# Moving start-up work between ScalarE and VectorE, and within VectorE's queue, in a transform-and-feed-forward kernel

## Chip, core, metric

The kernel runs on one core of a Trainium2 chip. The metric is the device time of one execution in microseconds (us). The kernel before takes 629.54 us (median of three runs, 629.07 to 629.83). In the views of the profile PE is TensorE's matmuls, PEld its weight loads, DVE is VectorE, ACT ScalarE, POOL GpSimd, and SP the engine that issues most DMAs. "L216" is line 216 of the kernel; the changed kernel's lines are about four higher than those of the kernel before.

## The reference

```
def _attn_ref(x):                       # x: 8 x 3008 x 256
    X = np.fft.fft(x, axis=1)
    X = np.fft.fft(X, axis=2)
    return X.real
def _moe_ref(x, w_gate, w_val, w_out):  # 24064 x 256, d_ff 1536
    gate = np.maximum(x @ w_gate, 0.0)
    val = x @ w_val
    return gate * val @ w_out
```

## The kernel before

The sequence transform is split into 94 x 32. For each of 8 batches, stage 1 multiplies by tables over 94 points, a turn brings the data onto other partitions, and stage 2 multiplies by tables over 32 points and yields `pq`. The transform over 256 columns is folded into the weights (`wc`, `ws`, `wm`), so that the main loop of 288 steps (8 batches, 3 blocks, 12 slices of d_ff) is gate, value, product and output matmuls. Batch 0 goes a special way, because nothing is there yet that could hide its start: its rows are multiplied as they land (`first_products`), with VectorE or ScalarE making the reversed copies (`ends`, `back`).

```python
def first_products(c, upper, k):            # row pair c, lower or upper x, straight or reversed copy
    ...
        nc.tensor.matmul(o, lhsT=lhs, rhs=other if k != upper else same, ...)                  # L216
        if jj == 0:                                                                           # self-paired row
            nc.tensor.matmul(psf[c][0:1, 384:480], lhsT=lhs[:, 0:1], rhs=..., ...)              # L219
...
pl.tensor_scalar(perm[:], dd[:], scalar1=mi[:], scalar2=None, op0=ALU.is_equal)   # POOL reads dd
...
jj, sl, up, odd = bits(0, 15), bits(4, 1), bits(5, 3), bits(0, 1)                 # DVE, 8 tiny ones
z = col("z", ...); nz = ...; mul = ...; o0 = ...; o1 = ...                        # DVE, 7 tiny ones
...
ends(24, 8); back(25, 3, "act"); back(28, 3, "dve"); ...                          # turn of the upper x
group((1, 2, 3), True)                                                            # PE: second half of rows 1 to 3
ends(8, 4); back(8, 4, "act")
dve.tensor_scalar(dd[:], dd[:], scalar1=mi[:], ...); residue(dd[:], dq[:], D, dve)
first_evac(2, "act"); first_evac(1, "dve"); first_evac(3, "dve")
...
fold_w(0, 0, 0, g_tile()); upright(0, 0, "act"); upright(0, 1, "dve")
fold_w(0, 0, 1, g_tile())                     # ends with the scaling of wm on DVE
rotate(0, 0, 4, dve.tensor_copy)
stage2(0, 0, 0, "act"); fold_w(0, 1, 0, g_tile()); stage2(0, 0, 1, "dve"); fold_w(0, 1, 1)
```

The remaining weight folds, and the uprights, rotations and stage 2 pieces of batch 0's blocks 1 and 2, are hung onto main-loop steps 1 to 10. They share two PSUM buffers in turn.

Of the kernel before, what the change touches and what calls it, by code (L numbers as in the profile page):

```python
# [11 lines left out]
F32 = mybir.dt.float32  # L12
# [32 lines left out]
def kernel(ctx: ExitStack, tc, x, w_gate, w_val, w_out, out):  # L45
# [9 lines left out]
    NKA = 12  # L55
# [136 lines left out]
    def back(r, n, evac):  # L192

        dst = tabs["back"][:, r:r + n, 1:H]
        src = free(xt[0]["lo" if r < NB // 2 else "hi"][0:NA], r % 16 * D + D - 1, [D, n], [-1, H - 1])
        if evac == "act":
            nc.scalar.copy(dst, src)
        else:
            nc.vector.tensor_copy(dst, src)

    def first_products(c, upper, k):

        if not (upper or k):
            psf[c] = early("ps1")
        for i in range(2):
            jj = 2 * c + i
            r = (NB // 2 if jj == 0 else NB - jj) if upper else jj
            o = psf[c][:, 192 * i:192 * i + 192]
            v = xt[0]["hi" if upper else "lo"][0:NA, r % 16, :]
            t = tabs["wn"]  # L210
            if jj:
                same, other = (free(t[:], 1536 + 96 * jj, [n, 2], [1, 96]) for n in (0, -1536))
            else:
                same, other = (free(wz[:], 96 * upper, [n, 2], [1, 96]) for n in (192, 384))
            lhs = tabs["back"][:, r, :] if k else v[:, 0:H]
            nc.tensor.matmul(o, lhsT=lhs, rhs=other if k != upper else same, start=not (upper or i or k),  # L216
                             stop=upper and i == 1 and k == 1, skip_group_check=True)
            if jj == 0:
                nc.tensor.matmul(psf[c][0:1, 384:480], lhsT=lhs[:, 0:1],  # L219
                                 rhs=wz[:, 0, int(upper), :] if k == upper else tabs["wzn"][:, int(upper), :],  # L220
                                 start=False, stop=upper and k == 1, skip_group_check=True)

    def first_evac(c, evac):

        if 0 not in t1t:
            t1t[0] = tp.tile([128, 16, D], BF16, tag="t1", bufs=1, name="t1")
        dst = free(t1t[0][:], 2 * c, [1536, 2], [16, 96], [1, 2])
        src = free(psf[c], 0, [96, 2], [1, 96], [192, 2])
        plain = nc.scalar.copy if evac == "act" else nc.vector.tensor_copy
        plain(dst, src)  # L230
        if c == 0:
            plain(free(t1t[0][0:1], 1536, [16, 96]), psf[0][0:1, 384:480])
# [84 lines left out]
    def pair_w(n, i, eng, parts=(0, 1)):  # L317
# [4 lines left out]
        if 1 in parts:  # L322
            eng.tensor_tensor(lo, lo, hi, op=ALU.subtract)

    def fold_w(n, i, cs, ps=None):

        ps = ps or spare("psw")
        for k, w in ((0, wst[i, n, 2]), (1, wst[i, n, 0])):
            nc.tensor.matmul(ps[64 * k:64 * k + 64, :], lhsT=cd[:, cs, 64 * k:64 * k + 64], rhs=w,  # L329
                             start=True, stop=True)  # L330
        sl_ = slice(n * 512, (n + 1) * 512)
        nc.scalar.copy((wc, ws)[cs][i][:, sl_], ps[:])  # L332
        if cs:
            nc.vector.tensor_scalar(wm[i][:, sl_], ps[:], scalar1=s2[:], scalar2=None, op0=ALU.mult)

    def nyquist():

# [6 lines left out]
    with tc.tile_pool(name="sp", bufs=1, space=SB) as sp:  # L344
        dve, pl = nc.vector, nc.gpsimd

        def residue(t, q, n, eng):

            eng.tensor_scalar(q, t, scalar1=1.0 / n, scalar2=RND, op0=ALU.mult, op1=ALU.add)
            eng.tensor_scalar(q, q, scalar1=-RND, scalar2=float(n), op0=ALU.add, op1=ALU.mult)  # L350
            eng.tensor_tensor(t, t, q, op=ALU.subtract)
# [8 lines left out]
        def absolute(out, a):  # L360
            nc.scalar.activation(out, a, ACTF.Abs)
# [16 lines left out]
        kbi = sp.tile([128, 4, NB], F32, tag="kbi")  # L378
        ui = sp.tile([128, 4, NB], F32, tag="ui")
        di = sp.tile([128, 4, 2, 16], F32, tag="di")  # L380
        ro = sp.tile([128, 4, 2, 16], F32, tag="ro")
        pi = sp.tile([128, 1], I32, tag="pi")
        npi = sp.tile([128, 1], F32, tag="npi")
        dve.memset(npi[:], -math.pi * (1.0 - 2e-7))
# [45 lines left out]
        def bits(shift, mask):  # L430
            ti = sp.tile([128, 1], I32, tag=f"b{shift}{mask}i")
            dve.tensor_scalar(ti[:], pi[:], scalar1=shift, scalar2=mask,
                              op0=ALU.logical_shift_right, op1=ALU.bitwise_and)
            tf = sp.tile([128, 1], F32, tag=f"b{shift}{mask}f")
            dve.tensor_copy(tf[:], ti[:])
            return tf

        def col(tag, a, *args, **kw):
            t = sp.tile([128, 1], F32, tag=tag)
            dve.tensor_scalar(t[:], a[:], *args, **kw)  # L440
            return t
# [20 lines left out]
        nc.scalar.mul(wn[:, 0, 9:16, :], wn[:, 1, 9:16, :], -1.0)  # L462
        nc.scalar.copy(w1[:, 1:10, :], wn[:, 1, 1:10, :])
        back(0, 2, "dve")
        jj, sl, up, odd = bits(0, 15), bits(4, 1), bits(5, 3), bits(0, 1)
        z = col("z", jj, scalar1=0.0, scalar2=None, op0=ALU.is_equal)
        nz = col("nz", z, scalar1=-1.0, scalar2=1.0, op0=ALU.mult, op1=ALU.add)
        mul = col("mul", z, scalar1=sl[:], scalar2=16.0, op0=ALU.mult, op1=ALU.mult)
        mul = col("mul2", mul, scalar1=jj[:], scalar2=None, op0=ALU.add)
        o0 = col("o0", nz, scalar1=sl[:], scalar2=-8.0, op0=ALU.mult, op1=ALU.mult)  # L470
        o0 = col("o1", o0, scalar1=8.0, scalar2=None, op0=ALU.add)
        o1 = col("o2", nz, scalar1=8.0, scalar2=o0[:], op0=ALU.mult, op1=ALU.add)
        dve.tensor_copy(cd[:, 1, 0:1], odd[:])
        dve.tensor_scalar(cd[:, 0, 0:1], odd[:], scalar1=-1.0, scalar2=1.0, op0=ALU.mult, op1=ALU.add)

        sv, ti = [], []
        tis = sp.tile([128, 2, 4, NB], I32, tag="m2i")
        for cs in range(2):
            ti.append(tis[:, cs])
            sv.append(sp.tile([128, 4, NB], F32, tag=f"m2s{cs}", name="sv"))  # L480
            pl.tensor_scalar(ti[cs], kbi[:], scalar1=mul[:], scalar2=(o0, o1)[cs][:], op0=ALU.mult, op1=ALU.add)
        pl.tensor_scalar(ui[:], ui[:], scalar1=up[:], scalar2=-1.0, op0=ALU.is_equal, op1=ALU.mult)

        ends(24, 8)
        back(25, 3, "act")
# [3 lines left out]
        group((1, 2, 3), True)  # L489
        ends(8, 4)  # L490
        back(8, 4, "act")
        dve.tensor_scalar(dd[:], dd[:], scalar1=mi[:], scalar2=None, op0=ALU.mult)
        residue(dd[:], dq[:], D, dve)
        first_evac(2, "act")
        first_evac(1, "dve")
        first_evac(3, "dve")
        dve.tensor_scalar(tis[:], tis[:], scalar1=NB - 1, scalar2=None, op0=ALU.bitwise_and)
        absolute(dq[:], dd[:])
        cosines(cd[:, 0, 1:H], dq[:, 1:H], D)
        sines(cd[:, 1, 1:H], dd[:, 1:H], D, 1.0)  # L500
        dve.tensor_scalar(tabs["wzn"][:], wz[:, 0], scalar1=-1.0, scalar2=None, op0=ALU.mult)

        group((4, 5), False)
        warm(4)
# [4 lines left out]
        back(12, 4, "act")  # L509
        ends(16, 4)  # L510
        back(16, 4, "dve")
        group((6, 7, 0), False)
        first_evac(4, "act")
        nc.sync.dma_start(out=seen[:], in_=t1t[0][0:1, 0, 8:10])
# [11 lines left out]
        for cs in range(2):  # L526
# [2 lines left out]

        iota(pl, di[:], [[-32, 4], [-16, 2], [-1, 16]], 0, 1)  # L530
        pl.tensor_scalar(s2[:], mi[:], scalar1=1.0, scalar2=-2.0, op0=ALU.min, op1=ALU.mult)
        pl.tensor_scalar(ro[:, :, 0, 1:16], di[:, :, 0, 1:16], scalar1=16.0, scalar2=-1.0,
                         op0=ALU.is_equal, op1=ALU.mult)
        pl.tensor_scalar(ro[:, :, 1, 1:16], di[:, :, 1, 1:16], scalar1=-16.0, scalar2=None, op0=ALU.is_equal)
        pl.tensor_scalar(ro[:, :, :, 0], di[:, :, :, 0], scalar1=0.0, scalar2=None, op0=ALU.is_equal)
        pl.tensor_copy(rot[:], ro[:].rearrange("p u s j -> p (u s j)"))
        pl.iota(ix[:], pattern=[[-1, 2], [4 * NA, B]], base=4 * NA - 1, channel_multiplier=-4)
        pl.tensor_scalar(ix[:], ix[:], scalar1=0, scalar2=None, op0=ALU.max)

        def g_tile():  # L540
            return psg.tile([128, 512], F32, tag="g", name="psw")

        pair_w(0, 1, pl)
        fold_w(0, 0, 0, g_tile())
        upright(0, 0, "act")
        upright(0, 1, "dve")
        fold_w(0, 0, 1, g_tile())
        rotate(0, 0, 4, dve.tensor_copy)
        stage2(0, 0, 0, "act")
        fold_w(0, 1, 0, g_tile())  # L550
        stage2(0, 0, 1, "dve")
# [4 lines left out]
        pair_w(1, 1, pl)  # L556
        for i in range(2):
            pair_w(2, i, pl)
        load_x(1, 1, nc.sync)
        first = fold(1, pl)  # L560
        for k in range(3):
            next(first)
        pl.dma_start(out=wo[:], in_=view(w_out, 0, [[D, 128], [128 * D, NF], [1, D]]))
        for k in range(3, FIRST):
            next(first)
# [174 lines left out]
    for n in (1, 2):  # L740
        for k, t in enumerate(((1, 2, 2, 3), (4, 5, 6, 7))[n - 1]):
            at(t, fold_w, n, k // 2, k % 2)
    for t, blk, cs, e in ((1, 1, 1, "dve"), (3, 1, 0, "dve"), (4, 2, 1, "dve"), (6, 2, 0, "dve")):
        at(t, upright, blk, cs, e)
    at(3, rotate, 0, 4, 8)
    at(6, rotate, 0, 8, NKA)
    for t, blk, cs, e in ((5, 1, 1, "dve"), (8, 2, 1, "act"), (9, 1, 0, "dve"), (10, 2, 0, "act")):
        at(t, stage2, 0, blk, cs, e)
    at(8, nyquist)

# [104 lines left out]
```

## Time and profile before

| stretch (us) | what runs | PE busy | what PE lacks |
|---|---|---|---|
| 6 to 14 | stage 1 of batch 0, first rows | 6.40 of 8 | rows not yet turned, a PSUM buffer not yet free |
| 14 to 24 | rest of stage 1, first folds | 9.64 of 10 | little |
| 24 to 54 | steps 0 to 11 with folds | 27.3 of 30 | PSUM buffers, VectorE |
| from 54 | main loop | 35.84 of 36 in the first stretch | nothing |

The table comes from the view of busy time by stretch, whose lines stand in the prediction.

### The profile page before, as it was taken

To read this page: it belongs to the slowest core of one execution; us is meant where nothing else is said; L and a number is where in the kernel's file an instruction comes from. 1 tells how busy PE (TensorE), PEld (TensorE's weight loads), DVE (VectorE), ACT (ScalarE), POOL (GpSimd) and SP (SyncE) were. 2 spreads that over 40 slices of the span, in tenths; PEclk is the share of its full clock that TensorE was granted. 3 is DMA by queue.
4 is the path that set the end of the run, shared out by engine and by line. 5 is a ranking of instruction groups with operands and counts; after the bars stand their busy time and mean duration, and the time that the engine had idled before them with its cause. 6 is when DMAs were issued, how large, how long until landed. Compare 5 with 4: busy or idle time off the path is not lost.

```text
span 626.9 us, 11935 instructions
## 1 busy us (share of the span) xinstructions
PE 613.0 (98%) x4252; PEld 408.9 (65%) x4284; DVE 538.8 (86%) x656; ACT 444.2 (71%) x852; POOL 520.0 (83%) x447
## 2 busy tenths in 40 slices
PE   7999999999999999999999999999999999999996
PEld 4335766666666666667666666766667666666665
DVE  8677888998889998888988988899988889899991
ACT  7557777777777768777777767777677777766660
POOL 8976998998989988988989989898988865565665
PEclk9999999999999999999999999999999999999999
DMA  7985166614744173722825155441732124212114
GB/s 167 234 159 123 32 164 156 148 33 128 181 104 107 45 206 79 169 47 83 212 60 143 43 151 148 113 108 35 217 81 62 33 84 117 60 34 67 33 35 99
DMA packets 42596, 67.44 MB, mean 108 GB/s; under 512 B 5871, under 2 KB 32520, under 8 KB 40520
## 3 DMA queue, kind: packets, MB, share of 16 engines
q1 hardware_dynamic: 37944, 51.38, 32.8%
q0 software_dynamic: 4432, 15.11, 10.2%
q8 instruction: 33, 0.54, 0.4%
q10 hardware_dynamic: 160, 0.20, 0.1%
q14 instruction: 27, 0.22, 0.1%
HBM read 38.85 MB, written 30.17 MB: 110 GB/s over the span
## 4 chain that ended last, share of the span: by engine, by line
PE 93%; DMA 3%; DVE 1%; issue 1%; ACT 1%; POOL 1%; POOLq 0%; DVEq 0%; ACTq 0%
PE po L678 39%; PE V L629 18%; PE G L614 10%; PE G L621 9%; PE G L615 9%; PE ps L162 2%; PE psw L329 2%; PE ps L271 2%; DMA lo<-in_x_dram 1%; DMA Td<-t 1%; DMA t<-Td 1%; PE ps L216 1%; DVE h L642 0%; ACT ws L332 0%; PE ps L166 0%
## 5 line engine op out<-in xcount | busy, mean ns | idle before, releaser
L649 POOL TENSOR_TENSOR h<-gm,E 128x992 bf16<-128x992 f32 (+1 forms) x138 | 319.9, 2318 | 84.7 <-DVE E L656 55.2
L678 PE MATMUL po<-wo,h 128*128 128x256 bf16 (+2 forms) x2304 | 328.6, 272 | 0.5
L678 PEld LDWEIGHTS <-h 128*128 128x128 bf16 (+2 forms) x2304 | 231.3, 103 | 105.9
L623 ACT ACTIVATE gm<-G 128x496 f32<-128x496 f32 (+1 forms) x288 | 170.4, 592 | 94.3 <-PE G L621 86.6
L642 DVE TENSOR_TENSOR h<-gs,V 128x1024 bf16<-128x1024 f32 (+3 forms) x150 | 173.8, 1159 | 59.5 <-PE V L629 42.3
L636 DVE SCALAR_TENSOR_TENSOR E<-nb,af,V 128x496 f32<-128x496 bf16 (+1 forms) x276 | 190.2, 730 | 1.2 <-PE po L678 1.2
L616 ACT ACTIVATE gs<-G 128x497 f32<-128x497 f32 (+2 forms) x288 | 169.6, 589 | 25.1 <-PE G L615 25.0
L656 DVE SCALAR_TENSOR_TENSOR E<-E,V 128x992 f32<-128x992 f32 (+1 forms) x138 | 164.4, 1191 | 0.0
L614 PE MATMUL G<-pq,wc 128*128 128x497 bf16 (+2 forms) x288 | 108.0, 375 | 1.2
L621 PE MATMUL G<-pq,wm 128*128 128x496 bf16 (+1 forms) x288 | 107.9, 375 | 0.3 <-ACT gs L616 0.3
L615 PE MATMUL G<-pq,ws 128*128 128x497 bf16 (+2 forms) x288 | 107.9, 375 | 0.0
L629 PE MATMUL V<-pq,ws 128*128 128x512 bf16 (+2 forms) x279 | 83.5, 374 | 0.3 <-DVE E L636 0.3
L629 PE MATMUL V<-pq,wc 128*128 128x496 bf16 (+2 forms) x266 | 80.7, 374 | 0.0
L615 PEld LDWEIGHTS <-ws 128*128 128x128 bf16 x288 | 28.2, 98 | 32.6
L691 ACT COPY os<-po 128x512 f32<-128x512 f32 x63 | 36.9, 586 | 14.6 <-PE po L678 13.2
L629 PEld LDWEIGHTS <-wc 128*128 128x128 bf16 x288 | 28.2, 98 | 20.2 <-issue 2.1
L114 POOL TENSOR_TENSOR eo<-xla 94x256 bf16<-94x256 f32 x56 | 40.2, 729 | 0.8
L614 PEld LDWEIGHTS <-wc 128*128 128x128 bf16 x288 | 28.2, 98 | 18.6 <-issue 1.3
L114 POOL TENSOR_TENSOR eo<-xlb 94x256 bf16<-94x256 f32 (+1 forms) x42 | 34.4, 820 | 0.9
L111 POOL TENSOR_TENSOR xla<-xla,xha 94x510 f32<-94x510 f32 x28 | 32.9, 1174 | 2.2
L177 ACT CAST t<-ps 96x512 bf16<-96x512 f32 x56 | 32.7, 583 | 2.4 <-PE ps L162 0.2
L621 PEld LDWEIGHTS <-wm 128*128 128x128 bf16 x288 | 28.1, 98 | 6.0 <-issue 3.4
(142 smaller groups left out, 368.1 us busy)
## 6 DMA issues: line engine op xcount, KB each, us to landing
out_dram<-os SPq DMA_DIRECT2D x124, 128.0 KB
Td<-t SPq DMA_DIRECT2D x7, 768.0 KB
t<-Td SPq DMA_DIRECT2D x7, 768.0 KB
out_dram<-os SPq DMA_DIRECT2D x82, 64.0 KB
xla<-in_x_dram SPq DMA_DIRECT2D x7, 720.0 KB
xlb<-in_x_dram SPq DMA_DIRECT2D x7, 640.0 KB
nb<-Nd SPq DMA_DIRECT2D x23, 128.0 KB
out_dram<-os SPq DMA_DIRECT2D x40, 48.0 KB
```

Source lines behind the costliest of these rows:

```text
L114: yield eng.tensor_tensor(e1[:, :, k:k + H], x1[:, :, 0:H], free(x1, D, [DX, n], [-1, H]), op=op)
L614: nc.tensor.matmul(G[:, ds], lhsT=wc[0][:, fs], rhs=pq[:, 0, ds], start=True, stop=False)
L615: nc.tensor.matmul(G[:, ds], lhsT=ws[0][:, fs], rhs=pq[:, 1, ds], start=False, stop=True)
L616: nc.scalar.activation(pair(t, "gs")[:, t % 2, ds], G[:, ds], ACTF.Relu)
L621: nc.tensor.matmul(G[:, cols], lhsT=wm[0][:, f * 128:(f + 1) * 128], rhs=pqt[b, blk][:, 1, cols], start=False, stop=True, skip_group_check ...
L623: nc.scalar.activation(pair(t, "gm")[:, t % 2, cols], G[:, cols], ACTF.Relu)
L629: nc.tensor.matmul(pair(t, "V")[:, t % 2, cs], lhsT=w[:, f * 128:(f + 1) * 128], rhs=pqt[b, blk][:, min(k, 1), cs], start=(k == 0), stop=( ...
L636: nc.vector.scalar_tensor_tensor(pair(t, "E")[:, t % 2, cols], nbt[b, blk][:, cols], af[:, f:f + 1], pair(t, "V")[:, t % 2, cols], op0=ALU ...
L642: nc.vector.tensor_tensor(pair(t, "h")[:, k, 0, 0:ds.stop - ds.start], pair(t, "gs")[:, k, ds], pair(t, "V")[:, k, ds], op=ALU.mult)
L649: eng.tensor_tensor(free(pair(t, "h")[:], 1024 * (t % 2) + 512 + w - 1, [1024, n], [-1, w]), pair(t, "gm")[:, k, cols], val[:, k, cols], o ...
L656: nc.vector.scalar_tensor_tensor(E[:, :, cols], E[:, :, cols], 2.0, V[:, :, cols], op0=ALU.mult, op1=ALU.subtract)
L678: nc.tensor.matmul(po[0:m, i, :], lhsT=pair(t - f + ff, "h")[:, ff % 2, sg, g * 128:g * 128 + m], rhs=wo[:, ff, :], start=(ff == 0), stop= ...
```

## The change

It intends a shorter start-up: ScalarE takes three evacuations from VectorE (B), VectorE's small work is put elsewhere in its queue (A), the self-paired row loads full-width weights (C), a scaling moves behind a rotation's copy (D), uprights and rotations move to steps where a PSUM buffer should be free (E, F), and the second half of batch 1's x is asked for later (G).

```diff
-                nc.tensor.matmul(psf[c][0:1, 384:480], lhsT=lhs[:, 0:1],
+                nc.tensor.matmul(psf[c][:, 384:480], lhsT=lhs,                       # C
...
         back(0, 2, "dve")
+        dve.tensor_scalar(dd[:], dd[:], scalar1=mi[:], scalar2=None, op0=ALU.mult)   # A
+        residue(dd[:], dq[:], D, dve)
         jj, sl, up, odd = bits(0, 15), bits(4, 1), bits(5, 3), bits(0, 1)
-        z = col("z", ...)   ... o1 = col("o2", ...)            # seven, now after first_evac(3)
...
-        dve.tensor_scalar(dd[:], dd[:], scalar1=mi[:], scalar2=None, op0=ALU.mult)
-        residue(dd[:], dq[:], D, dve)
-        first_evac(2, "act")
-        first_evac(1, "dve")
-        first_evac(3, "dve")
+        for c in (1, 2, 3):                                                          # B
+            first_evac(c, "act")
...
+        psw = g_tile()
+        fold_w(0, 0, 1, psw)
         rotate(0, 0, 4, dve.tensor_copy)
+        scale_w(0, 0, psw)                                                           # D
...
-    for t, blk, cs, e in ((1, 1, 1, "dve"), (3, 1, 0, "dve"), (4, 2, 1, "dve"), (6, 2, 0, "dve")):
+    for t, blk, cs, e in ((1, 1, 1, "dve"), (4, 1, 0, "dve"), (6, 2, 1, "dve"), (8, 2, 0, "dve")):   # E, F
         at(t, upright, blk, cs, e)
-    at(6, rotate, 0, 8, NKA)
+    at(7, rotate, 0, 8, NKA)
-    for t, blk, cs, e in ((5, 1, 1, "dve"), (8, 2, 1, "act"), (9, 1, 0, "dve"), (10, 2, 0, "act")):
+    for t, blk, cs, e in ((5, 1, 1, "act"), (9, 2, 1, "act"), (10, 1, 0, "dve"), (11, 2, 0, "act")):
```

Also moved: `ui`'s product from POOL to DVE, `rot` written without a cast, `ix` and `load_x(1, 1)` later on POOL (G), and the cosines and sines of `cd` behind a later turn.

More of the change, by code (lines that the diff above doesn't have):

```diff
@@ L323, in pair_w, with scale_w @@
             eng.tensor_tensor(lo, lo, hi, op=ALU.subtract)
+    def scale_w(n, i, ps):
+        nc.vector.tensor_scalar(wm[i][:, n * 512:(n + 1) * 512], ps[:], scalar1=s2[:], scalar2=None, op0=ALU.mult)
     def fold_w(n, i, cs, ps=None):
@@ L332, in fold_w @@
         nc.scalar.copy((wc, ws)[cs][i][:, sl_], ps[:])
-        if cs:
-            nc.vector.tensor_scalar(wm[i][:, sl_], ps[:], scalar1=s2[:], scalar2=None, op0=ALU.mult)
+        if cs and (n or i):
+            scale_w(n, i, ps)
     def nyquist():
@@ L380 @@
         di = sp.tile([128, 4, 2, 16], F32, tag="di")
-        ro = sp.tile([128, 4, 2, 16], F32, tag="ro")
         pi = sp.tile([128, 1], I32, tag="pi")
@@ L464 @@
         back(0, 2, "dve")
+        dve.tensor_scalar(dd[:], dd[:], scalar1=mi[:], scalar2=None, op0=ALU.mult)
+        residue(dd[:], dq[:], D, dve)
         jj, sl, up, odd = bits(0, 15), bits(4, 1), bits(5, 3), bits(0, 1)
-        z = col("z", jj, scalar1=0.0, scalar2=None, op0=ALU.is_equal)
-        nz = col("nz", z, scalar1=-1.0, scalar2=1.0, op0=ALU.mult, op1=ALU.add)
-        mul = col("mul", z, scalar1=sl[:], scalar2=16.0, op0=ALU.mult, op1=ALU.mult)
-        mul = col("mul2", mul, scalar1=jj[:], scalar2=None, op0=ALU.add)
-        o0 = col("o0", nz, scalar1=sl[:], scalar2=-8.0, op0=ALU.mult, op1=ALU.mult)
-        o0 = col("o1", o0, scalar1=8.0, scalar2=None, op0=ALU.add)
-        o1 = col("o2", nz, scalar1=8.0, scalar2=o0[:], op0=ALU.mult, op1=ALU.add)
-        dve.tensor_copy(cd[:, 1, 0:1], odd[:])
-        dve.tensor_scalar(cd[:, 0, 0:1], odd[:], scalar1=-1.0, scalar2=1.0, op0=ALU.mult, op1=ALU.add)
-        sv, ti = [], []
-        tis = sp.tile([128, 2, 4, NB], I32, tag="m2i")
-        for cs in range(2):
-            ti.append(tis[:, cs])
-            sv.append(sp.tile([128, 4, NB], F32, tag=f"m2s{cs}", name="sv"))
-            pl.tensor_scalar(ti[cs], kbi[:], scalar1=mul[:], scalar2=(o0, o1)[cs][:], op0=ALU.mult, op1=ALU.add)
-        pl.tensor_scalar(ui[:], ui[:], scalar1=up[:], scalar2=-1.0, op0=ALU.is_equal, op1=ALU.mult)
         ends(24, 8)
@@ L491 @@
         back(8, 4, "act")
-        dve.tensor_scalar(dd[:], dd[:], scalar1=mi[:], scalar2=None, op0=ALU.mult)
-        residue(dd[:], dq[:], D, dve)
-        first_evac(2, "act")
-        first_evac(1, "dve")
-        first_evac(3, "dve")
-        dve.tensor_scalar(tis[:], tis[:], scalar1=NB - 1, scalar2=None, op0=ALU.bitwise_and)
-        absolute(dq[:], dd[:])
-        cosines(cd[:, 0, 1:H], dq[:, 1:H], D)
-        sines(cd[:, 1, 1:H], dd[:, 1:H], D, 1.0)
+        for c in (1, 2, 3):
+            first_evac(c, "act")
+        z = col("z", jj, scalar1=0.0, scalar2=None, op0=ALU.is_equal)
+        nz = col("nz", z, scalar1=-1.0, scalar2=1.0, op0=ALU.mult, op1=ALU.add)
+        mul = col("mul", z, scalar1=sl[:], scalar2=16.0, op0=ALU.mult, op1=ALU.mult)
+        mul = col("mul2", mul, scalar1=jj[:], scalar2=None, op0=ALU.add)
+        o0 = col("o0", nz, scalar1=sl[:], scalar2=-8.0, op0=ALU.mult, op1=ALU.mult)
+        o0 = col("o1", o0, scalar1=8.0, scalar2=None, op0=ALU.add)
+        o1 = col("o2", nz, scalar1=8.0, scalar2=o0[:], op0=ALU.mult, op1=ALU.add)
+        sv, ti = [], []
+        tis = sp.tile([128, 2, 4, NB], I32, tag="m2i")
+        for cs in range(2):
+            ti.append(tis[:, cs])
+            sv.append(sp.tile([128, 4, NB], F32, tag=f"m2s{cs}", name="sv"))
+            pl.tensor_scalar(ti[cs], kbi[:], scalar1=mul[:], scalar2=(o0, o1)[cs][:], op0=ALU.mult, op1=ALU.add)
         dve.tensor_scalar(tabs["wzn"][:], wz[:, 0], scalar1=-1.0, scalar2=None, op0=ALU.mult)
+        dve.tensor_copy(cd[:, 1, 0:1], odd[:])
+        dve.tensor_scalar(cd[:, 0, 0:1], odd[:], scalar1=-1.0, scalar2=1.0, op0=ALU.mult, op1=ALU.add)
+        dve.tensor_scalar(ui[:], ui[:], scalar1=up[:], scalar2=-1.0, op0=ALU.is_equal, op1=ALU.mult)
         group((4, 5), False)
@@ L511 @@
         back(16, 4, "dve")
+        dve.tensor_scalar(tis[:], tis[:], scalar1=NB - 1, scalar2=None, op0=ALU.bitwise_and)
+        absolute(dq[:], dd[:])
+        cosines(cd[:, 0, 1:H], dq[:, 1:H], D)
+        sines(cd[:, 1, 1:H], dd[:, 1:H], D, 1.0)
         group((6, 7, 0), False)
@@ L531 @@
         pl.tensor_scalar(s2[:], mi[:], scalar1=1.0, scalar2=-2.0, op0=ALU.min, op1=ALU.mult)
+        ro = rot[:].rearrange("p (u s j) -> p u s j", u=4, s=2)
         pl.tensor_scalar(ro[:, :, 0, 1:16], di[:, :, 0, 1:16], scalar1=16.0, scalar2=-1.0,
@@ L535 @@
         pl.tensor_scalar(ro[:, :, :, 0], di[:, :, :, 0], scalar1=0.0, scalar2=None, op0=ALU.is_equal)
-        pl.tensor_copy(rot[:], ro[:].rearrange("p u s j -> p (u s j)"))
-        pl.iota(ix[:], pattern=[[-1, 2], [4 * NA, B]], base=4 * NA - 1, channel_multiplier=-4)
-        pl.tensor_scalar(ix[:], ix[:], scalar1=0, scalar2=None, op0=ALU.max)
         def g_tile():
@@ L543 @@
         pair_w(0, 1, pl)
+        pl.iota(ix[:], pattern=[[-1, 2], [4 * NA, B]], base=4 * NA - 1, channel_multiplier=-4)
+        pl.tensor_scalar(ix[:], ix[:], scalar1=0, scalar2=None, op0=ALU.max)
         fold_w(0, 0, 0, g_tile())
@@ L546 @@
         upright(0, 1, "dve")
-        fold_w(0, 0, 1, g_tile())
+        psw = g_tile()
+        fold_w(0, 0, 1, psw)
         rotate(0, 0, 4, dve.tensor_copy)
+        scale_w(0, 0, psw)
         stage2(0, 0, 0, "act")
@@ L558 @@
             pair_w(2, i, pl)
-        load_x(1, 1, nc.sync)
         first = fold(1, pl)
-        for k in range(3):
-            next(first)
+        next(first)
+        load_x(1, 1, pl)
+        next(first)
+        next(first)
         pl.dma_start(out=wo[:], in_=view(w_out, 0, [[D, 128], [128 * D, NF], [1, D]]))
```

## The prediction

The sum of this prediction comes to -0.6 us (+1.07 - 0.34 - 1.12 - 0.4 + about 0.2).

> **What bounds the kernel now.** I read the page first (shares of the engines, the 40 slices), then a table of busy time by stage, then the timeline and the chain of waits of the first 60 us, because everything the diff touches lies there.
>
> ```profile
> PE 613.0 (98%) x4252; PEld 408.9 (65%) x4284; DVE 538.8 (86%) x656; ACT 444.2 (71%) x852; POOL 520.0 (83%) x447
> ...
> PE   7999999999999999999999999999999999999996
> ```
>
> TensorE (PE) is busy 98% of the span, and only the first and last of 40 slices are loose. By stage (columns: stretch, its length, then busy us and instruction counts of PE, PEld, DVE, ACT, POOL):
>
> ```profile
> 6.00:14.00 8.00, 6.40 (x50) 4.17 (x52) 7.08 (x40) 6.40 (x15) 7.59 (x18) 1.00 1.02 220
> 14.00:24.00 10.00, 9.64 (x70) 4.29 (x68) 5.43 (x13) 6.28 (x14) 9.32 (x12) 1.00 0.76 251
> 24.00:35.00 11.00, 9.61 (x48) 3.25 (x48) 7.83 (x13) 6.20 (x13) 8.49 (x8) 1.00 1.10 214
> 35.00:54.00 19.00, 17.71 (x106) 7.20 (x105) 14.14 (x24) 12.26 (x24) 16.98 (x26) 1.00 0.72 133
> 54.00:90.00 36.00, 35.84 (x247) 24.65 (x249) 30.90 (x36) 26.62 (x50) 29.26 (x27) 1.00 0.38 93
> ```
>
> From 54 us on PE has almost no hole (35.84 of 36), so the rest of the run simply follows the instant at which step 12 starts on PE. The change can win only PE holes before 54 us: 1.60 + 0.36 + 1.39 + 1.29 = 4.6 us after the 6th, and of these some are warm-up and input waits. The time is therefore a question of when the matmul of step 12 starts (the last V matmul of step 11 stands at 53.21).
>
> The timeline shows which holes matter, and the order in which engines reach them:
>
> ```profile
> 8.36 0.61 POOL L412 TENSOR_SCALAR perm<-dd,mi 128x128 bf16<-128x128 f32 x1
> ...
> 9.30 0.22 DVE L189 COPY back<-hi 94x8 bf16<-94x8 bf16 x1
> ...
> 10.32 0.28 DVE L492 TENSOR_SCALAR dd<-dd,mi 128x128 f32<-128x128 f32 x1
> ...
> 11.53 1.01 DVE L230 CAST t<-ps 128x384 bf16<-128x384 f32 x2
> ...
> 12.14 0.33 PE L216 MATMUL ps<-wn,lo 94*128 94x192 bf16 x2 [1.01 <-DVE t L230]
> ...
> 14.99 0.20 PE L219 MATMUL ps<-wz,lo 94*1 94x96 bf16 x1
> ```
> ```profile
> 20.98 0.75 DVE L334 TENSOR_SCALAR wm<-psw,s 128x512 bf16<-128x512 f32 x1 [1.02 <-ACT ws L332]
> 21.64 0.17 DVE L260 CAST t<-psr 128x4 bf16<-128x4 f32 x1
> ...
> 34.42 0.17 PE L259 MATMUL psr<-t,rot 128*128 128x4 bf16 x1 [1.14 <-DVE wm L334]
> ...
> 42.79 0.17 PE L259 MATMUL psr<-t,rot 128*128 128x4 bf16 x1 [0.35 <-ACT wc L332]
> ...
> 53.21 0.37 PE L629 MATMUL V<-pq,wm 128*128 128x496 bf16 x1 [0.54 <-DVE h L642]
> ```
>
> To see: at 12.14 PE has stood for 1.01 us because DVE evacuated batch 0's stage 1 late; at 21.64 the first rotation's copy stood behind the scaling of a weight tile; at 34.42 and 42.79 a rotation needed a PSUM buffer that a weight tile still held; at 53.21 DVE is what PE waits for.
>
> [...] The changed line L219 goes from 1 to 128 columns. [...] the chain of waits gives each L219 0.13 us against 0.10 for its 128-column neighbours. [...] the 0.17 us copy had its input at about 20.4 and went after the 0.75 us scaling. [...] the hole at 34.42 is just a late evacuation, 1.14 us.
>
> **The change part by part.** Durations are those of the timeline above.
>
> A. Multiplying dd and its residue moves ahead of the input turns, and the column scalars move behind them. On paper this is neutral for DVE: 1.29 us in (10.32 to 11.61) for 1.2 us out. But dd is still read by POOL for perm (8.36 to 8.97), and the compiled order keeps dd's multiplication behind it: its wait asks for the POOL count that perm raises. So DVE now idles from 6.94 to about 9.03, then does the residue to 10.32 and the four bit fields (0.99 before, 6.86 to 7.85) to 11.31. Only then does it turn the upper x, which landed at 9.30: done 11.74 instead of 9.73. PE starts the second half of rows 1 to 3 at 11.80 instead of 9.79: 2.0 us late.
>
> B. ACT evacuates rows 1, 2, 3. ACT is free (its last turn ended at 10.85), so row 1 goes as soon as its products are there, about 12.55, done 13.1 (0.50 each, 0.4 to 0.45 when back to back). PE takes row 5's buffer at 13.15 instead of 12.14. So of A's 2.0 us half is recovered: PE is 1.0 late. Then, as before, 0.65 of matmuls and 0.87 of warm-up: 14.67 instead of 13.66. DVE, rid of two evacuations (1.0 us) but carrying the scalars (1.2), wzn (0.2) and the ui product (0.3, taken from POOL where it took 0.85), has the next turn ready at about 14.5: in time.
>
> C. Row 4's evacuation on ACT now comes after a turn (0.61) and abs, cosine, sine (0.94): about 13.9 + 0.6 + 0.95 = 15.45, done 16.0. Before, it ended at 14.76 and released PE at 14.82. So PE is 1.2 late. Full-width L219 gives back 4 x 0.03 = 0.12. At the first weight fold PE is then about 18.66 instead of 17.59: +1.07 us.
>
> D. The scaling behind the rotation: the copy can go at about 21.4 on the shifted clock, before the weight fold in PE's order has ended (22.55), so PE doesn't wait; before, it stood from 21.53 to 21.87. Gain 0.34. Lateness at step 0 is +0.7.
>
> E. Uprights and rotations in other steps. In step 3 the rotation now takes the buffer that the copy of a finished fold frees early (ACT 30.66 to 31.24): the hole from 33.30 to 34.42 goes, gain 1.12. In step 6 and 7 likewise 0.4. Following the two alternating buffers through steps 4 to 8 (fold's scaling on DVE ends about 35.05, 40.2, 45.3; PE asks at 35.1, 40.3, 45.3) I find every buffer free just in time. At the end of step 8 PE would be at about 46.1 instead of 47.2, with one more stage 2 (0.23) left: 0.86 ahead.
>
> F. But steps 9 to 11 have no weight folds, so PE needs only about 1.3 to 1.5 us a step while DVE needs 2 x 0.67 = 1.34 plus what is put there. The change puts an upright copy (0.69) and, later than before, a stage 2 copy (0.68) there, and moves one copy to ACT in step 5 where DVE had room. DVE then holds PE in steps 10 and 11 (0.5 + 0.3), and the last V of step 11 comes at about 52.65 instead of 53.21.
>
> Sum: +1.07 - 0.34 - 1.12 - 0.4 + about 0.2 = -0.6 us (sections A to F, rounded).
>
> G. On POOL, one cast of rot (0.70) and ui (0.85) go, but the input of tis comes 1.5 us later, so the pair sums start at about 16.6 instead of 17.04; nothing on PE waits for this. The second x half is asked for after the first turn, so the first x half should land sooner than 35.95 (POOL waits 3.04 us for it now); POOL pays about 1.3 us more issue time. Its consumer, stage 1 of batch 1, runs without PE waits now, so this is worth nothing in time.
>
> **Rivals.**
> R1: no stall in A, DVE busy exactly until 9.3 as the author of the order seems to have meant. For it: 6.94 + 1.29 + 0.99 = 9.22, which fits the landing of x too well to be chance. Against it: the semaphore count. If right, the +1.07 becomes about -0.6 (row 1 leaves at 11.4 instead of 12.03, and with it all that waits) and the kernel gains 2.3 us: 627.2.
> R2: steps 9 to 11 become DVE-bound enough that all of E is lost[...]. For it: 53.21 already waits for DVE. Then only A to D count: +0.7, 630.2.
> R3: the later x makes POOL late for batch 1's folds (three transfers now behind POOL's queue), so that stage 1 waits at 55 to 75 us. Against it: the landed half is needed only at 49.82, some 14 us after its new request, and the DMA view gives 7.5 and 8.6 us from issue to landing for such transfers. If it failed, 1 to 3 us slower, 631.
>
> **Range and chances.** -0.6 from 629.54 is 628.9; R1 has more weight than R2 and R3 together, since an order made on purpose usually does what it was made for, so I say 628.7. The range runs from R1 to R2, that is 627.2 to 630.1; three runs of before already spread over 0.8. Two per cent would be 12.6 us, and all holes before 54 us are 4.6, so faster by over 2% is all but impossible; slower by as much would need a stall none of these parts has.
>
> **What would show it.** Right: in the changed profile dd's multiplication starts right after perm at about 9.0, the turn of the upper x at 11.3, PE at 11.8, row 4's evacuation at about 15.4, the first fold at 18.7; no wait of a rotation for a PSUM buffer in steps 3 and 7; the last V of step 11 at about 52.6, waiting for DVE. Wrong: the turn at 9.3 (R1), the last V at 53.9 or later (R2), stage 1 matmuls waiting for POOL after 54 us (R3), or a difference that first appears after 90 us, where I expect none.

## The result

The changed kernel takes 628.1 us (median of four, 626.8 to 628.25) against 629.32 us (four runs of the kernel before). The ratio is 0.9975 with a 95% interval of 0.9958 to 0.9992. Ratios are the mean time of one kernel's fast runs over that of the other's fast runs of the same rounds, so they are not quite the ratio of the medians. The kernel is faster by a quarter of a per cent, well within 2%.

The profile after, first its shares of the engines on the page, then busy time by stretch with the same columns as in the prediction (the third number from the right is the granted clock of PE):

```profile
PE 615.6 (98%) x4284; PEld 409.9 (65%) x4284; DVE 537.5 (86%) x654; ACT 444.7 (71%) x855; POOL 520.1 (83%) x447
```
```profile
6.00:14.00 8.00, 5.87 (x44) 4.06 (x43) 5.48 (x35) 5.93 (x14) 6.43 (x15) 0.94 1.04 236
14.00:24.00 10.00, 9.90 (x74) 5.34 (x72) 5.70 (x16) 6.61 (x16) 7.57 (x12) 0.88 0.48 154
24.00:35.00 11.00, 10.75 (x51) 3.35 (x48) 6.91 (x13) 6.64 (x14) 9.09 (x8) 1.00 0.95 227
35.00:54.00 19.00, 17.98 (x111) 7.50 (x110) 15.24 (x26) 12.47 (x25) 17.41 (x26) 1.00 0.76 145
54.00:90.00 36.00, 36.00 (x251) 24.71 (x250) 30.90 (x36) 26.70 (x51) 31.57 (x30) 1.00 0.44 109
```

The page counts 4252 matmuls before and 4284 after, with 4284 weight loads in both, so 32 matmul records are missing before. PE's total busy time must not be compared; starts of instructions can be. The stretch from 24 us on is fuller than before, which fits part E (the rotation's hole of 1.14 us lay there). The stretch from 6 to 14 is emptier, and from 6 to 24 the clock is not 1.00, which I had not foreseen. The timeline of the changed kernel shows why (columns: start, us, engine, line, operation, then idle time before it and its releaser):

```profile
9.02 0.29 DVE L468 TENSOR_SCALAR dd<-dd,mi 128x128 f32<-128x128 f32 x1 [2.07 <-POOL perm L415]
...
11.07 0.17 DVE L189 COPY back<-hi 94x8 bf16<-94x8 bf16 x1
...
11.52 0.67 PE L216 MATMUL ps<-wn,hi 94*128 94x192 bf16 x6 [2.03 <-DVE hi L190]
...
13.85 1.91 PE L397 MATMUL psk<-wk 128*128 128x512 bf16 x4
...
16.67 0.91 ACT L230 CAST t<-ps 128x384 bf16<-128x384 f32 x2 [1.65 <-PE ps L216]
...
22.00 0.17 DVE L260 CAST t<-psr 128x4 bf16<-128x4 f32 x1 [0.43 <-PE psr L259]
...
22.60 0.75 DVE L327 TENSOR_SCALAR wm<-psw,s 128x512 bf16<-128x512 f32 x1 [0.42 <-ACT ws L336]
...
34.17 0.18 PE L259 MATMUL psr<-t,rot 128*128 128x4 bf16 x1
...
52.87 0.37 PE L633 MATMUL V<-pq,wm 128*128 128x496 bf16 x1 [0.54 <-DVE h L646]
```

VectorE waits 2.07 us for POOL's `perm`, then makes the residue, and turns the upper x at 11.07 instead of 9.30. PE stands for 2.03 us. Then four warm-up matmuls take 1.91 us in the changed kernel; in the kernel before, three of the same kind stand in one line of the timeline:

```profile
12.85 0.81 PE L394 MATMUL psk<-wk 128*128 128x512 bf16 x3
```

The rotation at 34.17 no longer waits, and the rotation's copy at 22.00 stands ahead of the scaling at 22.60.

A table of when PE starts the same weight load in each trace shows where time went and came from. "Fill" and "A undone" are experiments below.

| PE event (us from the span's start) | before | after | after, hole filled | after, A undone |
|---|---|---|---|---|
| second half of rows 1 to 3 | 9.79 | 11.51 | 11.53 | 10.35 |
| first self-paired load (L219) | 14.99 | 17.22 | 15.58 | 14.69 |
| first weight fold | 17.52 | 19.13 | 17.49 | 16.60 |
| first gate, step 0 | 23.20 | 24.48 | 22.85 | 21.96 |
| gate of step 4 | 34.45 | 34.21 | 32.57 | 31.69 |
| first output matmul, step 12 | 54.07 | 53.71 | 52.08 | 51.19 |
| output matmul no. 400 | 155.67 | 155.18 | 154.17 | 153.59 |
| last weight load | 620.73 | 620.24 | 619.23 | 618.65 |

The changed kernel is 1.61 us late at the first fold and 0.36 us early at step 12; it keeps about that to the end.

### The profile page after: what moved, and what is told of

It is laid out like the page before. It is cut to its first block, busy times and chain, and to the rows that moved or that the text cites. A ratio compares the mean times of both kernels' runs of the same rounds, so it can differ in the third digit from the quotient of the medians.

```text
span 626.4 us, 11966 instructions
## 1 busy us (share of the span) xinstructions
PE 615.6 (98%) x4284; PEld 409.9 (65%) x4284; DVE 537.5 (86%) x654; ACT 444.7 (71%) x855; POOL 520.1 (83%) x447
## 4 chain that ended last, share of the span: by engine, by line
PE 93%; DMA 2%; POOL 2%; DVE 1%; issue 1%; ACT 1%; SPq 0%; POOLq 0%
PE po L682 40%; PE V L633 19%; PE G L618 9%; PE G L619 9%; PE G L625 9%; PE ps L162 2%; DMA xha<-in_x_dram,ix 2%; PE ps L271 2%; PE psw L333 1%; POOL hi L132 0%; DMA wst<-in_moe_w_gate_dram 0%; PE ps L216 0%; DVE h L646 0%; PE psk L397 0%; POOL lo L129 0%
## 5 line engine op out<-in xcount | busy, mean ns | idle before, releaser
L633 PE MATMUL V<-pq,wc 128*128 128x497 bf16 (+2 forms) x288 | 85.4, 375 | 0.0
L633 PE MATMUL V<-pq,ws 128*128 128x497 bf16 (+2 forms) x288 | 85.4, 375 | 0.0
```

Of the source, the lines that this page charges most:

```text
L633: nc.tensor.matmul(pair(t, "V")[:, t % 2, cs], lhsT=w[:, f * 128:(f + 1) * 128], rhs=pqt[b, blk][:, min(k, 1), cs], start=(k == 0), stop=( ...
```

## The experiments

Theory T: part A is a loss, because its multiplication must wait for `perm`. The hole that it makes on PE also costs granted clock. Everything else gains. The first rival says that the transfers and POOL's pair sums set the start, so that A is slack. All outputs were correct. Where an expectation speaks of a window of the clock, it means the stretch at half clock seen in the changed kernel's profile: 3.41 us, about 13.0 to 16.4, at a granted clock of 0.50.

**The changed kernel again (no edit).**

> The changed kernel as it is, repeated. Theory T: the 2.0 us hole of TensorE before the second half of rows 1 to 3 lets the granted clock fall to half for one window of 3.4 us in most runs (three of four showed a mean clock of 0.995 and 628.0 to 628.3 us, the fourth 0.997 and 626.8). It expects two groups of times about 1.3 us apart, the slower one with the lower mean clock. Rival C (chance): the 626.8 was noise; times then spread evenly with no tie to the clock.

Measured: 628.86, 628.60, 628.25, 628.17 and 626.87, 627.03 us, ratio 0.9973 (0.9959 to 0.9987). With the four runs of the result, seven of ten lie at 628.0 to 628.9 and three at 626.8 to 627.0, so there are two groups 1.3 us apart. The mean clock follows only roughly: the upper group has 0.995 in six runs and 0.997 in one, the lower 0.997, 0.998 and 0.998. The mean also counts low clock in the tail of the run, where nothing is left to compute (0.73 from 622.0 to 626.3 us in the changed kernel's first profile, with PE busy for 0.00 us), so it can't separate them cleanly.

**A undone.**

```diff
         back(0, 2, "dve")
-        dve.tensor_scalar(dd[:], dd[:], scalar1=mi[:], scalar2=None, op0=ALU.mult)
-        residue(dd[:], dq[:], D, dve)
         jj, sl, up, odd = bits(0, 15), bits(4, 1), bits(5, 3), bits(0, 1)
+        z = col("z", ...)   ... o1 = col("o2", ...)
...
         back(8, 4, "act")
+        dve.tensor_scalar(dd[:], dd[:], scalar1=mi[:], scalar2=None, op0=ALU.mult)
+        residue(dd[:], dq[:], D, dve)
```

> The changed kernel with part A undone: the angle table's multiplication and residue again after the first turns, the column scalars again before them. Theory T (the stall behind the permutation matrix on VectorE, plus the clock it costs, is the one losing part): the turn of the upper x at 9.3 instead of 11.07, row 4's evacuation at about 13.8 instead of 16.7, first weight fold at 16.6 instead of 19.1, no half clock before the end; 625.6 us, that is 2.5 below the changed kernel in its usual state. Rival R (the weight and x transfers or the pair sums on GpSimd set the first folds, so that earlier stage 1 products only wait): fold no earlier than 18, gain under 1 us, above 627.

Measured: 625.81 us (625.43 to 626.71), ratio 0.9940 (0.9927 to 0.9953). The first fold starts at 16.60 and no clock is lost. The rival falls. In this profile the upper x was turned at 9.87 rather than the expected 9.3, because it landed late (VectorE waited 0.74 us for the transfer); in three later runs with the same order the turn came at 8.84 to 9.05. The input's landing thus varies by about 1 us from run to run. The fold did not suffer from it, because ScalarE's turn of a later piece of x, which the fold follows, had to wait 0.16 us more for that piece:

```profile
12.79 0.62 ACT L197 COPY back<-lo 94x508 bf16<-94x508 bf16 x1 [0.16 <-DMA lo<-in_x_dram]
```

The fold starts 3.8 us after this turn. In the three later runs the turn starts at 11.77, 12.20 and 12.83 and the fold at 15.59, 16.01 and 16.63, each time 3.8 us after it; in two of them it waits for the transfer too. So with A undone a transfer can set the start, and that much of the rival remains; the first folds of two single profiles can differ by 1 us for this reason alone.

**The hole filled, nothing else.**

```diff
-        warm(9)
+        warm(17)
```

> The changed kernel with 8 more warm-up matmuls (17 instead of 9) in the TensorE hole from 9.5 to 11.5, nothing else. They end at about 11.2, before the upper x is turned, so they delay nothing. Theory T: no half clock after 6 us, warm-up of 4 matmuls after row 5 takes 0.87 instead of 1.71, first fold at about 18.0 instead of 19.1, 626.9 us in every run. Rival (the half clock is set by something else, for instance the start of the run): clock window stays, 628.1 us.

Measured: 627.21 us (626.65 to 627.48), ratio 0.9962, all five runs within 0.9 us; 627.21 against 628.21 in the same rounds. PE still starts rows 1 to 3 at 11.53. The view by stretch, first of the changed kernel, then of this one:

```profile
9.50:11.50 2.00, 0.00 (x0) 0.00 (x0) 1.76 (x14) 0.82 (x3) 2.00 (x4) 1.00 1.08 188
...
13.00:16.40 3.40, 3.40 (x16) 2.21 (x16) 3.21 (x14) 1.98 (x6) 3.25 (x6) 0.50 0.50 192
```
```profile
9.50:11.50 2.00, 2.00 (x10) 0.74 (x8) 1.76 (x14) 0.83 (x3) 2.00 (x5) 1.00 1.08 179
...
13.00:16.40 3.40, 3.30 (x33) 2.67 (x33) 3.24 (x15) 3.37 (x10) 3.25 (x6) 1.00 0.54 211
```

With useless matmuls in the hole the clock stays at 1.00, PE finishes 33 matmuls from 13.0 to 16.4 instead of 16, and the first fold starts at 17.49 instead of 19.13. One profile alone would not show that the filling saved the clock, since the clock is lost or kept as the run falls (see the last experiment); that all five runs lie near the changed kernel's lower group (626.8 to 627.0), and none in its upper one, does. So of the 2.4 us between the changed kernel and A undone (628.21 and 625.81 in the same rounds), 1.0 is the clock and 1.4 the stall itself.

**One column of weights again.**

```diff
-                nc.tensor.matmul(psf[c][:, 384:480], lhsT=lhs,
+                nc.tensor.matmul(psf[c][0:1, 384:480], lhsT=lhs[:, 0:1],
```

> The changed kernel with the self-paired row's four matmuls again on one column of weights. My prediction's step C gave the full width 4 x 0.03 = 0.12 us; comparing the two traces from row 4's evacuation to the first fold gives 0.6. If the width itself is worth 0.6: the stretch from the first self-paired matmul to the first fold is 0.6 longer than in the changed kernel, 628.7 us. If it is worth 0.12, and the rest came from the later start, 628.2.

Measured: 628.63 us, ratio 0.9983 (0.9967 to 0.9998), runs in two groups, 627.51 to 627.86 and 629.40 to 629.87, each about 1 us above that of the changed kernel. The timeline of this run around the first self-paired matmul, then the same of the changed kernel:

```profile
16.98 0.25 PE L216 MATMUL ps<-wz,lo 94*128 94x192 bf16 x1
...
17.16 0.08 PEld L219 LDWEIGHTS <-lo 94*1 94x1 bf16 x1 [0.16 <-issue]
17.16 0.20 PE L219 MATMUL ps<-wz,lo 94*1 94x96 bf16 x1
...
17.30 0.26 PE L216 MATMUL ps<-wn,lo 94*128 94x192 bf16 x1
```
```profile
17.23 0.24 PE L216 MATMUL ps<-wz,lo 94*128 94x192 bf16 x1
17.23 0.10 PEld L219 LDWEIGHTS <-lo 94*128 94x128 bf16 x1 [0.25 <-issue]
17.31 0.20 PE L219 MATMUL ps<-wz,lo 94*128 94x96 bf16 x1
...
17.35 0.24 PE L216 MATMUL ps<-wn,lo 94*128 94x192 bf16 x1
```

From start to start the self-paired matmul costs 0.18 + 0.14 with one column and 0.08 + 0.04 with 128, so 0.20 us each and 0.8 for four. The stretch from the first of these matmuls to the first fold is 2.71 against 1.90 us. The prediction had 0.12. The narrow load itself is no longer than the wide one (0.08 and 0.10 us), but it starts 0.18 us after the matmul ahead of it, while the wide one starts together with that matmul. The edit also narrows the output in PSUM to one partition; which of the two delays the load was not tested.

**The old steps (E and F undone).**

```diff
-((1, 1, 1, "dve"), (4, 1, 0, "dve"), (6, 2, 1, "dve"), (8, 2, 0, "dve"))   rotate at 7   stage 2 at 5, 9, 10, 11
+((1, 1, 1, "dve"), (3, 1, 0, "dve"), (4, 2, 1, "dve"), (6, 2, 0, "dve"))   rotate at 6   stage 2 at 5, 8, 9, 10
```

> The changed kernel with the uprights, the rotation of the last block and the stage 2 pieces of batch 0 in their old steps (parts E and F undone). Prediction: E gained 1.12 + 0.4 and F gave some back, 1.3 in all; from the first gate of step 4 to the last V of step 11 the two traces give 1.63. So this kernel should have the 1.1 us hole of a rotation behind a weight scaling in step 3 again and end 1.3 to 1.6 us above the changed kernel: 629.5 to 629.8 in the state with the half clock, 628.3 without. Rival R2 (the steps are worth nothing because VectorE takes it back in steps 9 to 11): 628.2 or less.

Measured: 630.03 us, ratio 1.0019 (1.0003 to 1.0036), 1.8 us above the changed kernel's usual 628.2 (other rounds). Against the run with G undone below, whose profile lost clock as well (a mean of 0.997, here 0.996) and had the same first fold (18.87 and 18.86), the last V's weight load of step 11 comes at 53.33 instead of 51.68, so 1.65 us later. Rival R2 of the prediction falls: with A in place, the new steps are what makes the change a gain at all.

**A alone, in the kernel before.** The edit is A's part of the diff in the kernel before; the column scalars and what needs them come after the three evacuations.

> The kernel before with part A alone: the multiplication of the angle table and its residue ahead of the first turns, the column scalars behind the first evacuations. Theory T: the turn of the upper x at about 11.1 instead of 9.3, a hole of about 1.9 us on TensorE, in most runs a half clock window around 13 us; the first weight fold 2 to 3 us later than 17.5, the kernel 1.5 to 3 us slower than the one before. Rival (the order of VectorE is slack at the start, since the input transfers decide): fold within 0.5 us of 17.5, same time.

Measured: 636.04 us (635.17 to 636.45), ratio 1.0104 (1.0087 to 1.0121). This is 7 us slower, over twice what I expected. The view by stretch shows the reason:

```profile
16.40:19.00 2.60, 2.31 (x14) 1.83 (x15) 2.23 (x9) 1.29 (x4) 2.32 (x5) 0.50 0.00 0
19.00:27.00 8.00, 8.00 (x38) 3.79 (x37) 2.28 (x5) 2.71 (x6) 6.78 (x9) 0.50 0.78 256
```

Here the clock was at half from 13.39 to 27.04 us, that is for 13.65 us instead of 3.41, and the first fold started at 22.88. A second hole of 1.07 us, in front of the next turn (16.69), fell into that time; whether that hole kept the clock low was not tested by itself. It is at best part of the reason: after 16.8 us PE shows no hole (8.00 busy of 8 in the second line), and the clock still stayed at half for another 10.2 us, while in the changed kernel's profile it was back after 3.41; the views by stretch of its repeat and of the one-column run give about 3.5.

**x asked for early (G undone).**

```diff
-        load_x(1, 1, pl)        # after the first turn on POOL
+        load_x(1, 1, nc.sync)   # before it
```

> The changed kernel with the second half of batch 1's x requested early and from the other queue, as before (part G undone). Prediction: worth nothing in time, since neither stage 1 nor the folds wait for it: 628.2 like the changed kernel in its two states, the first turn on GpSimd at about the same 35.5. Rival R3 (the later request relieves or delays something on TensorE): a difference of over 1 us, seen after 50 us.

Measured: 628.40 us, ratio 0.9986 (0.9969 to 1.0002). It is the changed kernel's time. POOL's first turn came at 37.30, not at about 35.5 as I had written: the later request does let the first half land 1.8 us earlier, but nothing on PE waits for it. The prediction's "worth nothing in time" holds, and R3 falls.

**Full width alone, in the kernel before.** The edit is the one-column edit turned round.

> The kernel before with the self-paired row on the full width of weights, nothing else. The one-column run gave 2.71 us from the first self-paired product to the first fold against 1.91 with the full width, that is 0.8 for four. So the first fold at 16.7 to 16.9 instead of 17.5, unless something else holds it (the weight pair sum on VectorE ends at 16.5); the kernel 0.6 to 0.8 us faster, 628.8. With the 0.12 of my prediction: 629.4.

Measured: 628.11 us against 629.06, ratio 0.9983 (0.9966 to 0.9999). The first fold starts at 16.80 instead of 17.52, so 0.72 us of the 0.8 arrive.

**A and B undone.**

```diff
-        for c in (1, 2, 3):
-            first_evac(c, "act")
+        first_evac(2, "act")
+        first_evac(1, "dve")
+        first_evac(3, "dve")
```

> The changed kernel with A undone, as in the second experiment, and B undone too: rows 1 and 3 of stage 1 are again evacuated by VectorE, row 2 by ScalarE. Theory T (B's worth is half of what A cost, step B of the prediction, and little without A): row 5's buffer free at about 12.1 instead of 11.9, first fold 0.3 to 0.5 us later, 626.2 against 625.8. If B is the real gain of the change: over 1 us later, above 627.

Measured: 625.98 us, ratio 0.9944 (0.9931 to 0.9958); the first fold at 16.63 against 16.60. Without A, the evacuations on ScalarE are worth nothing that these runs can tell. PE's wait for a late evacuation by VectorE, known from the kernel before (12.14), is back, but what sets the fold here is the transfer that ScalarE's turn waits for, as in the profile of A undone:

```profile
11.61 0.32 PE L216 MATMUL ps<-wn,lo 94*128 94x192 bf16 x2 [0.95 <-DVE t L230]
...
12.83 0.61 ACT L197 COPY back<-lo 94x508 bf16<-94x508 bf16 x1 [1.96 <-DMA lo<-in_x_dram]
```

Whether B would count where that piece lands early, as in the next run (turn at 11.77), was not measured.

**A undone, batch 1's turn one step later.**

```diff
-(25, 30, (31, 32, 33, 34, 35, 37))
+(25, 31, (32, 33, 34, 35, 36, 37))
```

> The changed kernel with A undone, and with batch 1's rotation and first stage 2 pieces one step later. In every trace TensorE waits 0.3 to 1.1 us at 89 to 92 us for batch 1's shuffle through memory. If that wait is the reason why the 2.5 us gained by step 12 are only 1.6 at 155 us, this gives 0.5 to 0.9 back: 625.1. If the transfer only moves the wait elsewhere: 625.8.

Measured: 625.73 us, ratio 0.9944 (0.9930 to 0.9957). PE's wait for the shuffle is gone, but the list of PE's waits from 26 to 160 us has another in its place (1.1 us for VectorE's `E`), and the timeline shows what `E` waited for, the row of stage 2 that is broadcast through memory, and that now also starts a step later:

```profile
102.13 1.37 DVE L640 SCALAR_TENSOR_TENSOR E<-nb,af,V 128x496 f32<-128x496 bf16 x2 [2.26 <-DMA nb<-Nd]
```

The rival was right: the transfer moved the wait.

**As before, and two copies from VectorE to ScalarE.**

```diff
-(8, 2, 0, "dve"))     (10, 1, 0, "dve")
+(8, 2, 0, "act"))     (10, 1, 0, "act")
```

> As the run before it, and ScalarE takes the copies of the last upright of step 8 and of the stage 2 piece of step 10, which VectorE makes in the changed kernel. Step F of the prediction says that VectorE holds TensorE in steps 9 to 11 (0.5 + 0.3 us, and the copy at step 8); if so, the last V of step 11 comes 0.5 to 0.9 us earlier than in the run before it and the time is 624.4. If ScalarE becomes the bound in its place: no gain.

Measured: 625.51 us (625.35 to 625.88), ratio 0.9941 (0.9927 to 0.9954). From the gate of step 0 to the last V of step 11 it takes 27.47 us in both this kernel and the one before it, so the copies on VectorE cost nothing. The timeline of this kernel around step 10:

```profile
46.90 0.67 DVE L653 TENSOR_TENSOR h<-gm,V 128x496 bf16<-128x496 f32 x1 [0.53 <-PE V L633]
47.49 0.66 DVE L646 TENSOR_TENSOR h<-gs,V 128x496 bf16<-128x496 f32 x1
48.68 0.67 DVE L653 TENSOR_TENSOR h<-gm,V 128x496 bf16<-128x496 f32 x1 [0.53 <-PE V L633]
```
```profile
48.20 0.37 PE L633 MATMUL V<-pq,wm 128*128 128x496 bf16 x1
```

The steps still come every 1.78 us, though VectorE now idles 0.53 us in each. It is a circle: the mirrored V matmul (48.20) can overwrite V only when the direct product (47.49 + 0.66) has read it; the mirrored product (48.68) needs that matmul; the next direct product stands behind the mirrored one. In the changed kernel the copies lie in that idle time, where they cost nothing. The circle is read from the timeline and the code; no run breaks it.

**B alone undone (A stays).** The edit is as in A and B undone, in the changed kernel.

> The changed kernel with B alone undone, so A stays: rows 1 and 3 of stage 1 are evacuated by VectorE again, row 2 by ScalarE. Without A, undoing B cost nothing (first fold 16.63 against 16.60). With A, VectorE makes two evacuations (1.0 us) before the scalars and the next turn, so the turn of the next upper x ends at about 14.9 instead of 13.9. Theory T2 (B is what keeps A from costing more: a second hole on TensorE at 14 to 15 us keeps the clock at half for more than one window, as in the run with A alone, where it stayed for 13.65 us): half clock for two windows or more, first fold at 20.5 or later, 630 to 633 us. Rival (A alone lost 7 us for other reasons, B is slack here too): one window, fold at 19.1 to 19.5, 628.2.

Measured: 628.16, 629.27, 627.83 and 628.21 us, ratio 0.9987 (0.9970 to 1.0005). My expectation of 630 to 633 was wrong. The profiled run lost no clock at all (1.00 in each stretch from 9.5 to 27 us). PE's hole before rows 1 to 3 was 1.64 us in it, against 1.90 to 2.32 in the six profiles that lost the clock; whether the length decides was not tested. Its first fold came at 18.63, 1.1 us later than with A and B and no lost clock (the filled hole, 17.49), and the second hole, 0.92 us, is there. So with A in place B is worth about 1.1 us at equal clock. Whether the clock is lost varies from run to run here too: the mean clock of the four is 0.999, 0.993, 1.0 and 0.996. Why A alone loses the clock for so long is not settled.

## Why the prediction was right, and where it was not

The time (628.7, range 627.2 to 630.1) held: 628.1. The parts held less well, and two errors cancelled.

- **The bound: right.** In the pair of profiles the lead at step 12 is 0.36 us and 0.49 at the end. (The two profiled runs took 628.72 and 628.2 us; the pair thus holds only 0.5 of the 1.2 us between the medians, because the profiled run of the kernel before was one of its shorter ones. The parts below are checked on the pair.) The bound is not exact in general: A undone leads the kernel before by 2.88 us at step 12 and by 2.08 us at 155 us, since batch 1's shuffle and what follows it make PE wait there.
- **A: right in kind, missing its larger cost.** The wait for `perm` (2.07 us), against R1, is there; PE started rows 1 to 3 at 11.52 (predicted 11.80), as the residue took 1.05 us rather than 1.29. The step failed in taking a hole on PE to cost only its own length. It also cost the clock: half speed for 3.41 us, 1.64 us at the first fold, and 1.0 us in the medians.
- **B: right.** About half of A's delay was recovered: row 5's buffer was taken 0.80 us late (predicted 1.0). At equal clock and with A in place B is worth 1.1 us at the first fold. Without A nothing of it can be told, since the fold then waits for a transfer.
- **C: the mis-sized term.** Full width was given 4 x 0.03 = 0.12 us and measured 0.8. I read 0.13 against 0.10 from the chain of waits, which holds the time after an instruction; half of the cost of the one-column load stands before it, in the 0.24 of the matmul ahead, because that load starts late. Why it starts late no run shows; by itself it takes 0.08 us. Row 4's evacuation came at 16.67 instead of 15.45, behind PE at a clock of 0.50 (ScalarE waited 1.65 us for PE) and not behind ScalarE's queue.
- **First fold:** predicted +1.07, measured +1.61. Without the clock (filled hole) it is -0.03: the missing clock term (+1.64) was in part hidden by the undersized width (0.68) and by a further 0.42 that A to C cost less than I had thought. That the total came out near is luck to that extent.
- **D: right, by the traces.** The lateness fell from 1.61 to 1.28, so 0.33 (predicted 0.34). D was not undone by itself; from the first fold to the first gate it takes 5.35 to 5.36 us in the changed kernel and in all its variants but the two whose fold came first (5.57 and 5.60), against 5.69 in the kernel before.
- **E: right.** The rotation at 34.17 waits for nothing; from the fold of step 3 to the gate of step 4 the lateness of 1.28 turns into a lead of 0.24, of which 0.33 is only an upright put off. E and F together measured 1.65 us at step 11 between two like profiles (predicted 1.3 from the sum).
- **F: right effect, wrong cause.** The last V of step 11 waits for VectorE (52.87; predicted 52.65). But not for its load: moving the copies to ScalarE changes nothing, and the step time is a circle of 1.78 us through PE and VectorE.
- **G: right** (earlier undo: same time).

The version that beats both kernels is the changed one with A undone: 625.8 us, 0.6% faster than the kernel before, 0.4% faster than the changed one. The two further variants (0.9944, 0.9941) can't be told from it.

## What to carry to other kernels

Before moving work into an idle stretch of an engine's queue, ask what else reads the tile it overwrites: the idle time of VectorE was free, but the table was not. VectorE stood for 2.07 us, and the turn behind came at 11.07, though its piece of x had landed by 9.00, when ScalarE began on it. Don't take a hole on TensorE to cost only its length: in the changed kernel's profile one of 2.03 us was followed by 3.41 us at a clock of 0.50; a few useless matmuls in a hole that cannot be closed gave 1.0 us back here. And a wait for an engine does not show that the engine is overloaded: look whether it idles in the same period, as VectorE did for 0.53 us of 1.78 here.
